# First batch's down-projection sums moved from SBUF to DRAM with accumulating DMAs, and a new set of order offsets

## The chip, the cores and the metric

The kernel runs on one core of one Trainium2 chip. The metric is the device time of one launch in microseconds (us), and what is compared is the median of several runs. A profiled execution is one further launch; its trace gives, for every instruction, the engine, the start, the duration and what ended the idle time before it. TensorE is called PE here, VectorE DVE, ScalarE ACT, GpSimd POOL, and SyncE, which issues nearly all DMAs, SP.

## What is computed

Block-local attention with pooled far keys is followed by a gated feed-forward network. There are 4 batches of 768 tokens, 8 heads of 64, and a hidden width of 1536.

```python
scores_l = scale * np.matmul(q, k.transpose(0, 1, 3, 2))          # only |i-j| < 16 survives the mask
scores_s = scale * np.einsum('bhsd,bhnd->bhsn', q, k_sum) + np.log(block)   # k_sum: max of 32 keys
a = np.exp(scores_all - max); a = a / (sum + 1e-09)               # over both kinds together
x = np.matmul(a, np.concatenate([v, v_sum], axis=2))              # v_sum: mean of 32 values
g = x @ w_gate; silu = g * (1.0 / (1.0 + np.exp(-g)))
out = silu * (x @ w_val) @ w_out
```

The weights come as 64-bit floats. The kernel turns their bits into two float32r parts (high and low), and each product is taken as three matmuls: low by high, high by low, high by high.

## The kernel before

**The program is a list of steps.** `Plan.add` records every step with the engines that may run it, an estimate of its cost on each, and what it reads and writes. `order` then runs a list scheduler (`run`, lines 288 to 388 of the code) over the steps. For each engine it picks the step with the smallest value in the table `late`, which is worked back from when PE wants its operands. `nudge` adds offsets from the table `NUDGES` to that value: `+20.3` makes a step less urgent, `a`, `d` or `p` pins it to ACT, DVE or POOL, and `s1.3` sets how long a PE step of the attention is held back. The engines of the chip then run their own lists strictly in order. A step that waits holds everything behind it on its engine, and a DMA that waits holds the DMAs behind it on SP.

**Work on PE.** Two lists are merged: the feed-forward network (the main line) and the attention of the next batch (the side line). A batch has two halves of 384 tokens (`k` counts halves over all batches: 0 and 1 are batch 0) and four pairs of heads (`u`).

- The side line has the scores `SC(k,u)`, the transposes `PP0/PP1(k,u)` and the attention results `XO(k,u)`.
- Around them stand the pooling of keys and values (`pool`, `vpool`, tiles `ks`, `vr`), maxima and exponentials, the normalisation `nrm` (tile `p`), evictions of the transposes `pt0/pt1`, copies of values (`odd`, `val`, `values`, tile `vw`) and the split of the result into high and low parts `xh/xl` (tiles `xh_B`, `xl_B`).
- In batch 0 the main line does `g(j,hf)` and `v(j,hf)` at line 1014 for each of 12 blocks of hidden units `j` and each half. `silu`, `mul`, `hh`, `hl` follow on the other engines.
- In batches 1 to 3 a seven-product scheme at line 1038 replaces them: `P1(b,j)` to `P7(b,j)`, with sums `s1`, `s7`, `u2`, `vv`, `c12`, `c21`, `c22` taken by ACT, DVE and POOL. `P3` writes over the bank that `vv` reads, so it waits for `vv`.
- After each three `j`, `down` (line 1108) multiplies by `w_out`. For each of six groups of 128 tokens `t`, the steps `D0(b,g,t)` and `D1(b,g,t)` add into one PSUM bank `acc`; `g` is 0 to 3.

**Weights.** In batch 0 each block `j` is decoded: a DMA `raw_w`, then `abs`, `clamp`, `shift`, `sign` (L913), `low` (L919), `hi` and `lo`, after which `w_j` can be used by `g(j,0)`. Four sums `sumA..` follow, and two DMAs `sf(j)` and `wa(j)` keep decoded weights in DRAM. `w_out` is decoded in the same way (`o0` to `o10`). In batch 1, `la(1,j)` and `ls(1,j)` load `wa` and `sf` again, and `sh(j)` and `sl(j)` split the second one. Loads go into four slots, so `ls(1,j)` waits until an earlier block's slot is free.

**Sums of the down-projection.** `finish` (in `down`) takes the bank `acc` when `D1` is done. For `g` = 0 a copy puts it into the SBUF tile `part` (512 floats on 128 partitions, one tile for each `t`). For `g` = 1 to 3, DVE adds `acc` to that tile. After `g` = 3, SP stores the tile to the output. That holds for all four batches. The tiles lie in the pool `late`, which takes the place of the pool `pro` (first batch's data) when its last reader is done.

**Filling matmuls.** The program begins with 11 matmuls of a zero tile (`dummy`, 22 on PE). Before a PE step that the scheduler sees waiting more than half a microsecond in its first 110, `warm_up` puts up to 10 more (20 on PE).

Of the kernel before, what the change touches and what calls it, by code (L numbers as in the profile page):

```python
# [205 lines left out]
XO(0,2) s0.3; raw_w1 +25.9; max1(1,0) +3.5; eps(1,0) +4.9 d; raw_w2 +6.1; sign_w2 -120.3; sumA11_w2 -94.3 d
sumA12_w2 +63.7 p; vw(1,1) +44.9; max0(1,1) +42.9; scl0(1,1) +5.3; eps(1,1) -27.6 d; mul(1,0) +11.9
values(1,0) -18.1 p; pt1(1,0) +7.8 a; xl(0,1) +43.1; max0(1,2) -57.5; scl0(1,2) +130.9; eps(1,2) +44.3
mul(2,0) -15.7; values(1,1) -41 a; XO(1,1) s0.2; xh(1,1) +34 d; xl(1,1) -53.1; max0(1,3) -109.1; exp2(1,3) +22.1
exp3(1,3) +5.5; exp4(1,3) +47.8; eps(1,3) +121.7 p; raw_o0 +23.5; low_o0 +69.4; lo_o0 +58.3 d; raw_o2 +48.5  # L210
clamp_o2 +42.7; sign_o2 +45.2; raw_w3 +21; sumA11_w3 +28 d; sumA12_w3 +25.7 d; hl(0,3,0) -0.6 p; values(1,2) -20.1 a
xh(2,1) -22.5 d; xl(2,1) -26.5; hh(0,3,1) +12.7 d; sumA12_w4 +42.4; raw_o4 +35.9; hh(0,4,0) -12.1 d; kw(2,0) +115.8
vpool(1,0) +88.1; join(2,0) -32.5 p; kt(1,1) +70.8; pool(1,1) +78.9; ttr0(2,0) -54.6; ttr1(2,0) -49.1; SC(2,1) s1.3
ttr0(2,1) -55.2; ttr1(2,1) -123.6; eps(2,1) +41.2 p; silu(4,1) -103.9; mul(4,1) -59.5; hh(0,4,1) -34 d
hl(0,4,1) +64.3 d; clamp_w5 +65.2; shift_w5 +79.9; lo_w5 -50.4 d; wa5 +68.8; hh(0,5,0) +68.1; PP0(2,0) s3
vs(1,0) -17.4; pt1(2,0) +26.7 d; pt0(2,1) -53.5 a; values(2,0) +106.8; values(2,1) +67.6 p; hh(0,5,1) +6.8
vpool(1,2) +63.1; XO(2,0) s0.6; xf(2,0) +17 d; exp4(2,2) -57.9; exp5(2,2) -28.1; exp1(2,3) -93.2; exp2(2,3) -55.9
exp3(2,3) -123.9; exp4(2,3) +44.1; part(0,1,4) +39.9; part(0,1,5) +61.9; abs_w6 +81.1; shift_w6 +15.1
sumA22_w6 -0.2 p; sumA21_w6 +86.8; silu(6,0) +36.6; hl(0,6,0) -20.6 p; pt0(2,3) +18.3 d; PP1(2,3) s1.6
hl(0,6,1) -27.5 d; shift_w7 +106.2; sign_w7 +34.6; sumA11_w7 +27.6 d; sf7 +9.9; q(3,0) -160.7; kw(3,0) -21.8  # L220
join(3,1) +120.2; XO(2,2) s0.3; exp3(3,0) +15.5; ttr1(3,1) +16.1; nrm(3,1) -61.6 p; hh(0,7,1) +47.5 d
hl(0,7,1) +32 p; abs_w8 +79.9; sign_w8 -90.5; low_w8 +35.7; sumA21_w8 -69.7 d; sumA11_w8 -62.6 d; sumA12_w8 +72.7 p
raw_o8 +104; low_o8 +38.2; lo_o8 -29.4 d; silu(8,0) +33.7; hh(0,8,0) +45.2; hh(0,8,1) +73.3; pt0(3,1) -64.1 a
values(3,0) +21.6 d; q(3,3) +60.7; eps(3,2) -90.7 p; ttr1(3,3) +25.6; abs_w9 +28.3; sumA21_w9 -2 p
sumA11_w9 -28.4 p; wa9 +52.2; PP0(3,2) s2.4; values(3,2) +27.9 d; clamp_w10 +53.4; sumA21_w10 -106.3; raw_o10 +41.3
abs_o10 +10.3; clamp_o10 +111.7; shift_o10 +26.9; hh(0,10,1) +50.3 a; lo_w11 +20.7 p; sumA11_w11 -1.8 p
mul(11,0) -71.4; hl(0,11,0) +13; hl(0,11,1) +94.8; T3(1,0) -37; B11h(1,0) -55.1; B11l(1,0) -21.3 p; T2l(1,0) +53 p
T4h(1,0) +126.5; T4l(1,0) -61.4 p; B22h(1,0) -10.2; B22l(1,0) +87; T3(1,1) +75 d; B11h(1,1) -2.1 d; T3h(1,1) +42.1 d
T1h(1,1) +48.7 a; B21h(1,1) -29.9; B22h(1,1) -14.4; sh(0) +44; mul(1,0,0) -83.6 p; hh(1,0,0) -120.5 d
mul(1,0,1) +58.9 p; pool(2,0) +48.2; vpool(2,0) -58.2; q(4,1) +111.3; kw(4,1) +48.8; pool(2,1) +43.5  # L230
# [1170 lines left out]
```

## Time and profile before

| | us |
|---|---|
| median of 3 runs | 687.5 (687.2 to 690.58) |
| the profiled execution's own time | 690.92 |
| its span, from the first to the last instruction | 689.1 |
| PE busy | 673.0 |
| DVE busy | 515.4 |
| ACT busy | 352.0 |
| POOL busy | 96.8 |

HBM was read for 113.73 MB and written for 34.60 MB. The granted PE clock was 0.999. PE's busy time counts the filling matmuls. In a line of the timeline the columns are start, duration, engine, source line, operation and tiles, and in brackets the idle time of the engine just before and what ended it. A group's line gives the count, the busy time, the mean duration in ns and the idle time before.

### The profile page before, as it was taken

How to read it: one execution, taken by the hardware profiler on the slowest of the kernel's cores; microseconds unless marked ns; L12 is line 12 of the kernel's file. 1: busy time of each engine (PE TensorE's matmuls, PEld its weight loads, DVE VectorE, ACT ScalarE, POOL GpSimd, SP SyncE). 2: the span in 40 equal slices, each digit the busy share in tenths (PEclk: the TensorE clock that was granted, in tenths of full speed). 3: DMA queues.
4: the chain of work that ended last, by engine and by line, in shares of the span. 5: the costliest groups of instructions: out<-in, count | busy, mean ns of one | idle time of the engine just before them, and what ended most of it. 6: DMA issues, size and time to landing. Idle time of an engine off the chain costs nothing.

```text
span 689.1 us, 13426 instructions
## 1 busy us (share of the span) xinstructions
PE 673.0 (98%) x5156; PEld 621.2 (90%) x5156; DVE 515.4 (75%) x1141; ACT 352.0 (51%) x855; POOL 96.8 (14%) x109
## 2 busy tenths in 40 slices
...
GB/s 305 299 357 324 255 202 267 163 254 263 246 199 295 204 294 245 233 267 241 289 163 253 201 273 149 231 202 151 235 35 208 193 218 104 214 107 214 107 107 92
DMA packets 69471, 149.19 MB, mean 217 GB/s; under 512 B 22752, under 2 KB 45088, under 8 KB 62496
## 3 DMA queue, kind: packets, MB, share of 16 engines
...
HBM read 113.73 MB, written 34.60 MB: 215 GB/s over the span
## 4 chain that ended last, share of the span: by engine, by line
PE 75%; DMA 10%; DVE 10%; issue 2%; ACT 2%; POOL 1%; SPq 1%; ACTq 0%; POOLq 0%; DVEq 0%
PE p L1038 32%; PE acc L1108 25%; PE g L1014 5%; DMA s<-ss 4%; PE v L1014 4%; PE xo L710 3%; PE sc L561 2%; PE pp L677 2%; DMA sf<-m_w 2%; DMA kt<-in_kP 1%; DVE m_w L919 1%; DVE m_w L913 1%; DMA vt<-in_vT 1%; POOL m_w L447 1%; DMA wa<-wa 1%
## 5 line engine op out<-in xcount | busy, mean ns | idle before, releaser
L1108 PE MATMUL acc<-o,hh 128*128 128x512 f32 x576 | 179.4, 392 | 0.6 <-DVE o L447 0.6
L1108 PEld LDWEIGHTS acc<-o,hh 128*128 128x128 f32 x576 | 107.1, 188 | 23.2 <-DVE o L447 0.9
L1038 PE MATMUL p<-xh_T,s 128*128 128x384 f32 x432 | 122.8, 339 | 1.8 <-DMA s<-ss 1.3
L1108 PE MATMUL acc<-o,hl 128*128 128x512 f32 x288 | 112.5, 391 | 0.0
L1038 PE MATMUL p<-xh_B,wa 128*128 128x384 f32 x288 | 84.8, 335 | 0.0
L442 ACT COPY s<-p 128x384 f32<-128x384 f32 x64 | 30.8, 481 | 102.8 <-PE p L1038 102.8
L1038 PEld LDWEIGHTS p<-xh_T,s 128*128 128x128 f32 x432 | 79.0, 188 | 4.8 <-DMA s<-ss 3.1
L447 DVE TENSOR_TENSOR part<-acc,part 128x512 f32<-128x512 f32 x72 | 47.9, 688 | 33.2 <-PE acc L1108 33.2
L1038 PE MATMUL p<-xl_T,s 128*128 128x384 f32 x216 | 72.2, 334 | 0.0
L1108 PEld LDWEIGHTS acc<-o,hl 128*128 128x128 f32 x288 | 54.0, 188 | 11.5
L1014 PE MATMUL g<-xh_B,w 128*128 128x384 f32 x192 | 53.9, 341 | 3.2 <-DVE w L447 1.7
L604 ACT ACTIVATE p<-p,nm 128x120 f32<-128x120 f32 x144 | 55.1, 384 | 1.1 <-DVE nm L592 0.6
L447 DVE TENSOR_TENSOR c<-p,u 128x384 f32<-128x384 f32 x72 | 39.8, 554 | 20.4 <-PE p L1038 19.9
L447 DVE TENSOR_TENSOR hl<-a,hh 128x384 fp32r<-128x384 f32 x87 | 51.6, 595 | 3.4 <-ACT hh L442 0.6
L442 ACT CAST hh<-a 128x384 fp32r<-128x384 f32 x52 | 26.6, 515 | 53.0 <-DVE a L447 51.5
L1038 PEld LDWEIGHTS p<-xh_B,wa 128*128 128x128 f32 x288 | 53.0, 188 | 0.1
L1014 PE MATMUL v<-xh_B,w 128*128 128x384 f32 x192 | 52.9, 336 | 0.0
L1038 PE MATMUL p<-xl_B,wa 128*128 128x384 f32 x144 | 48.1, 334 | 0.0
L1038 PE MATMUL p<-xh_B,s 128*128 128x384 f32 x144 | 42.6, 336 | 2.1 <-DVE v L447 2.1
L447 DVE TENSOR_TENSOR a<-c,a 128x384 f32<-128x384 f32 x69 | 39.8, 580 | 4.7 <-ACT a L996 2.1
L1038 PE MATMUL p<-xh_T,wa 128*128 128x384 f32 x144 | 42.4, 335 | 0.0
L1038 PEld LDWEIGHTS p<-xl_T,s 128*128 128x128 f32 x216 | 40.6, 188 | 0.3
...
## 6 DMA issues: line engine op xcount, KB each, us to landing
...
s<-ss SPq DMA_DIRECT2D x24, 1024.0 KB, 7.4
raw_w<-in_wgv SPq DMA_DIRECT2D x12, 1024.0 KB, 6.0
ss<-s SPq DMA_DIRECT2D x12, 1024.0 KB, 5.5
...
```

The costliest lines, as they stand in the source:

```text
L442: nc.scalar.copy(out, in_)
L447: vector[e].tensor_tensor(out=out, in0=a, in1=b, op=op)
L561: nc.tensor.matmul(make(sc[h])[s * QT : (s + 1) * QT, c * KC + at : c * KC + at + x.shape[-1]], make(q)[hs, qs], x, start=not biased or c ...
L604: nc.scalar.activation(out=make(p)[:, i, :], in_=make(p)[:, i, :], func=AF.Exp, scale=-1.0, bias=make(nm)[:, i : i + 1], accum_out=make(sm ...
L677: nc.tensor.transpose(make(pp)[:KC, c * P : (c + 1) * P], make(p)[:, g * NT // 2 + c, :], make(id_sb))
L710: nc.tensor.matmul(ps[hs, qs], v, make(pt)[:, h, qs], start=True, stop=True)
L913: lambda e: nc.vector.scalar_tensor_tensor(out=bits(), in0=high(), scalar=-0x40000000, in1=bits(), op0=ALU.bitwise_and, op1=ALU.bitwise_or ...
L919: lambda e: nc.vector.scalar_tensor_tensor(out=bits(), in0=low(), scalar=29, in1=bits(), op0=ALU.logical_shift_right, op1=ALU.bitwise_or), ...
L1014: nc.tensor.matmul(t[:, :TOK], a, x, start=u == 0 and n == 0, stop=u == NP - 1 and n == 2)
L1038: nc.tensor.matmul(t[:, :TOK], a, x, start=first and kk == 0 and n == 0, stop=kk == 1 and n == 2, skip_group_check=not first,)
L1108: nc.tensor.matmul(ps, a, w, start=j == js[0] and m == 0, stop=j == js[-1] and m == 2)
```

## The change

There are four edits.

1. `SPILL = 1`: for batch 0, `finish` copies every `acc` into the SBUF tile (on ACT or DVE) instead of adding on DVE. For `g` = 0 a DMA of SP, `keep(0,t)`, writes the tile to a DRAM tile `sum`. For `g` = 1 to 3 a DMA issued by POOL, `plus(0,g,t)`, adds it to `sum` in DRAM. After `g` = 3, SP copies `sum` to the output. There are 6 `keep`, 18 `plus` and 6 `out` DMAs; batches 1 to 3 stay as they were. The SBUF tile is a new one of the same ring for each `g`, so the copy of one `g` waits until the DMA of the one before has read it.
2. `FIRST`: the scheduler's clocks begin at 5.4 for PE and 1.3 for DMA instead of 0.
3. The scheduler asks for the port shared by DVE and POOL only for steps that use it, since a `plus` does not.
4. Another table `NUDGES`, so that the whole order is another one. `ON_BANK = 2` is what `HALVES` was, and `parts_sb` and `id_r` move to the pool `cst`; neither changes an instruction.

```diff
+SPILL = 1
+ON_BANK = 2
...
+FIRST = {PE: 5.4, DVE: 0.0, ACT: 0.0, POOL: 0.0, DMA: 1.3}
...
+ISSUE = 1.2
...
-kt(0,1) -60.2; id_sb -72.2; vr(1) -12.4; kt(0,0) +8.2; kt(0,2) +20.3; pool(0,2) +97.4; vn(0) +23.7; bias_sb +35.4
+kt(0,1) -75.5; q(0,1) -42.6; raw_parts -146.9; id_sb -68.8; mean_sb -6.3; vn(1) -13.6; vr(1) -11.5; kt(0,3) -18.7
...
-    free = {PE: 0.0, DVE: 0.0, ACT: 0.0, POOL: 0.0, DMA: 0.0}
+    free = dict(FIRST)
...
-                    if x == POOL:
+                    if x == POOL and s.port:
...
+    def add_dma_sum(name, nbytes, out, in_, reads, writes):
+        plan.add(
+            name, {POOL: ISSUE}, lambda e: nc.gpsimd.dma_start(out(), in_(), accum_op=ALU.add), reads, writes, port=False
+        )
+        plan.add(f"{name}'", {DMA: nbytes / 0.33e6}, lambda e: None, reads, writes)
...
+            if b < SPILL:
+                part = buf("late", f"part{t}", [P, DM], f"part_{b}_{g}_{t}", room="late")
+                add_copy(f"part({b},{g},{t})", (ACT, DVE), DM, lambda: make(part), lambda: make(acc), (acc,), (part,), kind="evict")
+                if g == 0:
+                    to = PART[t] = buf("dram", f"sum{t}", [P, DM], f"sum_{b}_{t}")
+                    add_dma(f"keep({b},{t})", P * DM * 4, lambda: make(to), lambda: make(part), (part,), (to,))
+                    return
+                to = PART[t]
+                add_dma_sum(f"plus({b},{g},{t})", P * DM * 4, lambda: make(to), lambda: make(part), (part,), (to,))
+                if g == NJ // GROUP - 1:
+                    add_dma(f"out({b},{t})", P * DM * 4, lambda: out[r : r + P, :], lambda: make(to), (to,), ())
+                return
```

Where the order changes is shown at three places. The first is DVE in the opening stage, from the `sign` of the fourth weight block (tile `m_w_790`) to its `lo` (tile `w_931`), after which PE can begin `g(3,0)`. Before:

```order
L913 SCALAR_TENSOR_TENSOR m_w_790<-raw_w_481,m_w_790 128x1024
L614 TENSOR_REDUCE nm_2_867<-sc_1_2_823 128x3
L919 SCALAR_TENSOR_TENSOR m_w_790<-raw_w_481,m_w_790 128x1024
L447 TENSOR_TENSOR a_1_0_794<-v_0_742,a_1_0_794 128x384
L447 TENSOR_TENSOR xl_B_0_0_929<-xo_0_796,xh_B_0_0_862 128x384
L447 TENSOR_TENSOR m_w_735<-m_w_735 128x256
L444 CAST hh_1_0_937<-a_1_0_794 128x384
L447 TENSOR_TENSOR o_870<-m_o_613,o_870 128x1024
L447 TENSOR_TENSOR w_931<-m_w_790,w_931 128x1024
```

After the change the fourth block's tiles are `m_w_811` and `w_918`; `m_o` belongs to `o2` and `pt_1` to the transposes of `(1,1)`:

```order
L925 SCALAR_TENSOR_TENSOR m_w_811<-raw_w_471,m_w_811 128x1024
L626 TENSOR_REDUCE nm_2_885<-sc_1_2_831 128x3
L931 SCALAR_TENSOR_TENSOR m_w_811<-raw_w_471,m_w_811 128x1024
L453 TENSOR_TENSOR a_1_0_820<-v_0_731,a_1_0_820 128x384
L912 TENSOR_SCALAR m_o_867<-m_o_867 128x1024
L450 COPY pt_1_927<-pp_1_1_914 120x384
L450 COPY pt_1_927<-pp_1_1_920 120x384
L453 TENSOR_TENSOR w_918<-m_w_811,w_918 128x1024
```

The `lo` of `o0` and three small steps have left this stretch, and two evictions of transposes and a `clamp` have come in. On PE, the order here was `SC(1,3)`, `g(3,0)`, `v(3,0)`; now `SC(1,3)` stands between `g(3,0)` and `v(3,0)`.

The second place is DVE in the decoding of the eighth block, between the `shift` and the `lo` of `w7`. `vr_3` is the pooling of the values of `(1,3)`, whose load is `vt_3`; `part_4` and `part_5` release the PSUM banks of `D1(0,1,4)` and `D1(0,1,5)`. Before:

```order
L906 TENSOR_SCALAR m_w_1677<-m_w_1677 128x1024
L447 TENSOR_TENSOR part_3_1390<-acc_1_3_1749,part_3_1390 128x512
L782 TENSOR_REDUCE vr_3_1888<-vt_3_1851 128x24
L913 SCALAR_TENSOR_TENSOR m_w_1677<-raw_w_1449,m_w_1677 128x1024
L447 TENSOR_TENSOR part_4_1395<-acc_1_4_1832,part_4_1395 128x512
L919 SCALAR_TENSOR_TENSOR m_w_1677<-raw_w_1449,m_w_1677 128x1024
L447 TENSOR_TENSOR part_5_1411<-acc_1_5_1853,part_5_1411 128x512
```

After, from `part(0,1,4)` on (`vr_2` is the pooling for `(1,2)`; block `w7` is `m_w_1699`, and its `lo` writes `w_1937`):

```order
L450 COPY part_1_4_1890<-acc_1_4_1833 128x512
L453 TENSOR_TENSOR m_w_1672<-m_w_1672 128x256
L931 SCALAR_TENSOR_TENSOR m_w_1699<-raw_w_1447,m_w_1699 128x1024
L794 TENSOR_REDUCE vr_2_1929<-vt_2_1236 128x24
L665 RECIPROCAL ri_2_1934<-sm_2_1849 128x6
L912 TENSOR_SCALAR m_o_1738<-m_o_1738 128x1024
L450 COPY part_1_5_1942<-acc_1_5_1851 128x512
L918 TENSOR_SCALAR m_o_1738<-m_o_1738 128x1024
L453 TENSOR_TENSOR w_1937<-m_w_1699,w_1937 128x1024
```

The pooling of `(1,3)` no longer stands ahead of `part(0,1,4)` and of the `lo` of `w7`; it comes five rows behind that `lo`.

The third place is SP at the change from batch 0 to batch 1. `wa_2` and `s_2` are the loads `la(1,2)` and `ls(1,2)`. Before:

```order
L461 DMA out<-part_2_1183 128x512
L461 DMA ss_2942<-s_1_2861 128x2048
L461 DMA out<-part_3_1390 128x512
L461 DMA out<-part_4_1395 128x512
L461 DMA out<-part_5_1411 128x512
L461 DMA wa_2_3038<-wa_903 128x1536
L461 DMA s_2_3086<-sf_955 128x1024
```

After:

```order
L467 DMA ss_2907<-s_1_2803 128x2048
L467 DMA out<-sum_0_1157 16x4096
L467 DMA out<-sum_1_1168 16x4096
L467 DMA out<-sum_2_1228 16x4096
L467 DMA out<-sum_3_1387 16x4096
L467 DMA out<-sum_4_1407 16x4096
L467 DMA wa_2_3073<-wa_862 128x1536
L467 DMA s_2_3124<-sf_1127 128x1024
```

Five outputs still stand ahead of the two loads, and each of them now waits for the landing of a `plus` that POOL issues, not for an instruction of DVE; the sixth has moved behind.

More of the change, by code (lines that the diff above doesn't have):

```diff
@@ L206 @@
[L206 to L230, printed above, removed]
@@ L231 @@
-vpool(2,1) +49.5; vw(4,1) +27.4; exp3(4,0) -52.3; ttr1(4,1) -8.9; eps(4,1) -38.4 a; sl(1) -54.9 p; s1(1,1) -3.1 d
-vv(1,1) -37.2; mul(1,1,0) -38.8; c22(1,1) +85.3 d; pool(2,2) -145.4; pool(2,3) -132.1; ls(1,3) +8.5
+kt(0,1) -75.5; q(0,1) -42.6; raw_parts -146.9; id_sb -68.8; mean_sb -6.3; vn(1) -13.6; vr(1) -11.5; kt(0,3) -18.7
+q(0,3) -5.3; kt(0,2) +6.9; pool(0,2) +116.7; vn(0) +8.6; bias_sb -61.1; SC(0,3) s0.4412; exp1(0,3) +173.7
+nrm(0,3) +80.1 p; fv(3) -55.9; exp0(0,0) +98; exp2(0,0) -80.4; exp4(0,0) -50.6; exp5(0,0) -125.4; nrm(0,0) +73.2 p
@@ new lines @@
+rcp(1,1) -90.3; nrm(1,1) -18.5; hh(0,1,0) -12.1 a; hl(0,1,0) +77.7; pt1(1,0) -12 a; xh(0,1) -132.6 a; xl(0,1) -19.5
+SC(1,2) s2.7; max1(1,2) -70.3; exp4(1,2) +179; nrm(1,2) +65; hl(0,2,0) -60.5; pt1(1,1) -109.2 d; xh(1,1) -14.2 d
+scl0(1,3) +9.9; scl1(1,3) +119.9 a; eps(1,3) -116.8 p; nrm(1,3) +2.8 p; raw_o0 +8.4; lo_o0 +62.7; raw_o2 +51.9
+lo_o2 +40.8; raw_w3 +8.7; clamp_w3 -35.3; shift_w3 -13.3; sign_w3 -90.8; hi_w3 -61.1; sumA22_w3 +53.8 p
+hh(0,3,0) +11.9 d; hl(0,3,0) -39 p; PP0(1,2) s2.6; XO(1,2) s0.3391; keep(0,0) -45.2; keep(0,1) -69.7
@@ new lines @@
+hh(0,0,1) +102.5 a; hl(0,0,1) +84.5 d; hh(0,1,1) +14.6 a; hl(0,1,1) -152.2 p; hh(0,3,1) +42.4 a; sumA22_w4 +106.8 d
+sumA21_w4 -74 p; sumA12_w4 +48.4 d; raw_o4 +35.9; shift_o4 -29.8; lo_o4 -99 p; mul(4,0) +4.8; hh(0,4,0) +13.4 d
+pool(1,0) +57.6; vpool(1,0) +64.6; vw(2,0) -50.4; kw(2,1) +60.3; exp5(2,0) +15.8; SC(2,1) s2.5; ttr0(2,1) +31.5
+ttr1(2,1) +35.5; exp0(2,1) +5.2; eps(2,1) -57.3 p; hl(0,4,1) +64.7 d; shift_w5 -67.6; lo_w5 +34.5 p
+sumA22_w5 +15.2 d; silu(5,0) +90.6; PP0(2,0) s0; pt0(2,0) -34.7 d; vs(1,1) -42.2; values(2,1) -81.4 d
@@ new lines @@
+silu(5,1) -69.9; part(0,1,0) +31.5; vpool(1,2) +95.4; vpool(1,3) +133.8; join(2,3) -54.9 d; ttr1(2,2) -24
+eps(2,2) +9.3 p; nrm(2,2) +23.9 p; ttr0(2,3) -21.8; ttr1(2,3) +49.6; eps(2,3) +86.8; rcp(2,3) +56; nrm(2,3) +60.8 p
+part(0,1,4) +3.1 d; plus(0,1,4) -64.6; part(0,1,5) +161.8; sf6 +68.8; shift_o6 +13.3; silu(6,0) +50.4
+hh(0,6,0) -44.6 d; pt0(2,2) -122.8 d; pt1(2,2) +78.6 d; pt0(2,3) -76; abs_w7 +0.5; low_w7 +78.6; sumA21_w7 +98.9 p
+sumA11_w7 +65.3 p; hl(0,7,0) -36 d; q(3,0) +156.4; join(3,0) +41.2; XO(2,2) s0.7; ttr0(3,0) +65.2; ttr1(3,0) -91.8
```

32 lines of the change are left out of this document (22 added, 10 removed).

## The prediction

> **What bounds the kernel now.** I read the page first, then the busy time by stage, then the waits of PE, and last the timeline around each wait and the chain of waits. The page gives the span and the busy time of the engines.
>
> ```profile
> span 689.1 us, 13426 instructions
> PE 673.0 (98%) x5156; PEld 621.2 (90%) x5156; DVE 515.4 (75%) x1141; ACT 352.0 (51%) x855; POOL 96.8 (14%) x109
> ```
>
> PE is busy for 98% of the span, so the kernel as a whole is bound by PE. The change leaves the products as they are, so a gain can only come from the 2% in which PE is idle and from filling matmuls. The windows by stage show where that is. The columns are the window, its length, then busy time and count of PE, PE weight load, DVE, ACT and POOL, the granted clock, the DMA share and GB/s.
>
> ```profile
> 16.40:82.40 66.00, 61.65 (x795) 56.41 (x788) 65.20 (x113) 54.85 (x142) 22.86 (x25) 1.00 0.89 317
> 82.40:230.80 148.40, 146.03 (x1105) 134.38 (x1105) 131.20 (x281) 93.27 (x205) 45.57 (x45) 1.00 0.70 236
> 230.80:377.80 147.00, 144.35 (x1104) 134.09 (x1103) 114.04 (x285) 79.14 (x204) 15.79 (x20) 1.00 0.73 243
> ```
>
> In the opening (16.4 to 82.4) DVE is busy for 65.20 of 66.00 us: there DVE sets the time, and PE's busy time contains filling matmuls. In the rest of batch 0 (to 230.8) PE is idle for 148.40 − 146.03 = 2.37 us, in batch 1 for 2.65 us. Batches 2 and 3 keep their order of work nearly unchanged, and I give them nothing. PE's waits, summed by what ended them, name the pieces (total, times, longest):
>
> ```profile
> PE p L1038 <- DVE v L447: 2.1, 2, 1.4
> PE g L1014 <- DVE w L447: 1.7, 2, 0.9
> PE g L1014 <- DVE part L447: 1.0, 1, 1.0
> PE g L1014 <- ACT a L996: 0.6, 1, 0.6
> ```
>
> All of them are waits for an engine that runs its list in order, so each step that is moved on DVE can shift one of them.
>
> **The change, part by part.**
>
> **1. The opening.** Three rows of DVE's timeline show its two stalls near the start and the `lo` of `w3`; the chain of waits shows the two products of PE that need it.
>
> ```profile
> 13.80 0.95 DVE L500 TENSOR_REDUCE ks<-kt 128x24 f32<-128x768 f32 x1 [1.96 <-DMA kt<-in_kP]
> 16.09 0.29 DVE L444 COPY vs<-pv 24x128 f32<-24x128 f32 x1 [0.36 <-ACT vs L442]
> 62.38 1.21 DVE L447 TENSOR_TENSOR w<-m_w,w 128x1024 fp32r<-128x1024 f32 x1
> ```
>
> ```profile
> 65.15 2.16 PE g L1014 x12
> 67.31 2.08 PE v L1014 x12
> ```
>
> Between the second scale of `(0,3)` and the `lo` of `w3`, DVE's list had 80 steps and now has 85. Twelve have left it: two `nrm` (now on POOL), the pooling of `(1,0)`, three sums `sumA`, one `hh`, three copies of values and two `eps`. Seventeen have come in: four evictions `pt`, seven copies of values, `fv(2)`, a reciprocal, one `sumA`, one `clamp` and two `eps`. The prices, for the stretch from 10 to 66:
>
> ```profile
> L656 DVE TENSOR_TENSOR p<-p,ri 128x720 f32<-128x720 f32 x6 | 5.7, 956 | 0.1
> L447 DVE TENSOR_TENSOR m_w<-m_w 128x256 f32<-128x256 f32 x7 | 2.9, 414 | 0.0
> L444 DVE COPY vw<-vn 64x384 f32<-64x384 f32 x2 | 1.1, 549 | 0.1
> L444 DVE COPY pt<-pp 120x384 f32<-120x384 f32 x1 | 0.6, 551 | 0.0
> L900 DVE TENSOR_SCALAR m_o<-m_o 128x1024 f32<-128x1024 f32 x2 | 1.3, 668 | 0.0
> ```
>
> I set the small ones against each other (two `eps`, `hh` and a sum on the one side, two `eps`, `fv(2)`, the reciprocal and a sum on the other). Out remain 2 x 0.956 + 0.95 (as the pooling at 13.80) + 2 x 0.414 + 3 x 0.549 = 5.3; in come 4 x 0.551 + 7 x 0.549 + 0.668 = 6.7. Net 1.4 us more on an engine that is full. On the other side, the load that DVE awaits at 13.80 is now asked for ahead of one load of `q` (192 KB, an estimate of 0.6 us at the 317 GB/s of the opening), and the copy that waited 0.36 is another one. So the stretch starts about 1.0 earlier and `lo` of `w3` ends 0.4 later. From there PE has the same work, since `SC(1,3)` only changes place with `g(3,0)`. **I take +0.4.** Bounds: −1.0 if the five extra steps only fill gaps, +1.4 if no stall near the start shrinks.
>
> **2. Batch 0's sums.** By the order, 19 of the 24 evictions of `acc` stood on DVE and 5 on ACT; now 7 copies run on DVE and 17 on ACT.
>
> ```profile
> L447 DVE TENSOR_TENSOR part<-acc,part 128x512 f32<-128x512 f32 x72 | 47.9, 688 | 33.2 <-PE acc L1108 33.2
> L442 ACT COPY part<-acc 128x512 f32<-128x512 f32 x21 | 12.0, 587 | 16.6 <-PE acc L1108 15.8
> ```
>
> DVE is freed of 12 x 0.69 = 8.3 us, and ACT takes 12 x 0.587 = 7.0. ACT has 148.40 − 93.27 = 55 us free in that stage, DVE 17: the load itself is covered on both. If that cover is not there, the cost is a later `silu`, such as the 0.6 above. What the freed time is worth stands in PE's waits on DVE there:
>
> ```profile
> 143.21 0.95 DVE L782 TENSOR_REDUCE vr<-vt 128x24 f32<-128x768 f32 x1 [3.06 <-DMA vt<-in_vT]
> 149.91 1.23 DVE L447 TENSOR_TENSOR w<-m_w,w 128x1024 fp32r<-128x1024 f32 x1
> ```
>
> ```profile
> 145.95 0.44 PE L1014 MATMUL g<-xh_B,w 128*128 128x384 f32 x1 [0.98 <-DVE part L447]
> 151.19 0.44 PE L1014 MATMUL g<-xh_B,w 128*128 128x384 f32 x1 [0.80 <-DVE w L447]
> ```
>
> DVE stands 3.06 us for a load of values, and behind it wait `part(0,1,4)`, whose bank PE needs, and the `lo` of `w7`. Now that pooling stands behind both. The one that took its place reads a tile loaded much earlier. **I take −1.8** (0.98 + 0.80); the bound above is 0, if the two `m_o` steps and the DVE `sumA` that came in use up what is won. The 0.6 on ACT stays: 0, bound −0.6.
>
> **3. Eighteen accumulating DMAs from POOL, six `keep` and six `out`.** Of these the trace shows nothing alike: before, POOL issues no DMA of data. Nearest rows:
>
> ```profile
> L447 POOL TENSOR_TENSOR m_w<-m_w 128x256 f32<-128x256 f32 x27 | 27.1, 1005 | 86.5 <-DVE w L447 35.5 <-issue 28.1 <-DVE m_w L447 22.1
> raw_o<-in_wo SPq DMA_DIRECT2D x6, 1024.0 KB, 8.7
> sf<-m_w SPq DMA_DIRECT2D x12, 512.0 KB, 4.9
> out<-part SPq DMA_DIRECT2D x24, 256.0 KB, 2.1
> ```
>
> For one issue on POOL I take 1.0 us, its commonest step: 18 us more on an engine that has 103 us free in that stage and has lost 21 steps to others. For the landing of one `plus` of 256 KB I take 4.9, the row of a 512 KB write, since the tile is also read and added; bounds 2.1 and 8.7. In transfers the sums add 18 x 0.26 = 4.7 MB, and `keep` 1.6 MB, to the 236 GB/s x 148.4 us = 35 MB of that stage: the share of 0.70 would become 0.83, or 0.92 if each sum moves twice. Both are below 1, so 0.
>
> The place where a landing can reach PE is the end of batch 0. The rows are of DVE, SP's queue and PE.
>
> ```profile
> 231.37 1.28 DVE L447 TENSOR_TENSOR part<-acc,part 128x512 f32<-128x512 f32 x2
> ```
>
> ```profile
> 237.22 0.33 SPq L461 DMA_DIRECT2D wa<-wa  x1
> 238.27 0.33 SPq L461 DMA_DIRECT2D s<-sf  x1
> ```
>
> ```profile
> 246.97 0.34 PE L1038 MATMUL p<-xh_T,s 128*128 128x384 f32 x1
> ```
>
> `out(0,4)` waits on SP ahead of `la(1,2)` and `ls(1,2)`, and now for `plus(0,3,4)`. The copy ends at about 232.0, the issue adds 1.0, the landing T, and SP's two issues ahead of `ls` 0.33 each: `ls` could go at 233.7 + T instead of 238.27. Its product begins 0.16 after the last split of that load is done, so PE stalls for T − 4.8: 0.1 at T = 4.9, 0 at 2.1, 3.9 at 8.7. **I take +0.1.** The Trainium skill, page "DMA: Bandwidth & Descriptors", section on the anatomy of one DMA on the GpSimd path, fits such a DMA with 2.0 us plus its bytes at 436 GB/s; that would be 2.6 us for 256 KB (an estimate), and this term 0 instead of 0.1. No run of before shows it, and the fit says nothing of adding.
>
> **4. Batch 1.** DVE at 285 and 318, and PE there:
>
> ```profile
> 285.12 0.70 DVE L444 CAST s<-s 128x1024 fp32r<-128x1024 f32 x1 [2.85 <-DMA s<-sf]
> 318.08 0.95 DVE L500 TENSOR_REDUCE ks<-kt 128x24 f32<-128x768 f32 x1 [2.20 <-DMA kt<-in_kP]
> ```
>
> ```profile
> 286.33 0.45 PE L1038 MATMUL p<-xh_B,s 128*128 128x384 f32 x1 [1.36 <-DVE v L447]
> 287.93 0.45 PE L1038 MATMUL p<-xh_T,s 128*128 128x384 f32 x1 [0.28 <-DVE u L447]
> 319.56 0.44 PE L1038 MATMUL p<-xh_B,s 128*128 128x384 f32 x1 [0.72 <-DVE v L447]
> ```
>
> At 285, `sh(5)` waited 2.85 us for its load ahead of `vv(1,4)`; now `vv` stands ahead of it. But the load comes no sooner, and `P6(1,5)` needs `sl(5)`, so part of the 1.64 returns a few products later: **−0.6**, bounds −1.64 and 0. At 318 the pooling that waits for `kt` stood ahead of `vv(1,6)` alone; now `u2(1,6)` and a reciprocal stand ahead of `vv` too, the first about as long as a copy of 0.55, the second short: **+0.8**, bounds −0.7 (the load comes in time) and +0.8.
>
> **The sum:** +0.4 − 1.8 + 0 + 0.1 − 0.6 + 0.8 = −1.1. The profiled execution took 690.92 us, 3.4 above the median of 687.5 and within the runs shown (687.2 to 690.58) but for 0.3. I apply the difference to the median: **686.4 us**, no change that a measurement could tell; that takes about 0.5%, 3.4 us.
>
> **The rivals.**
>
> *A, faster.* The new list fits throughout: `vv` and the splits at 285 no longer meet, the opening's extra copies lie in gaps, and no DMA is late. Then go 1.0 (opening), 1.8, 0.6 (ACT) and 1.64: −5.0, so 682.5 us. For it speaks that DVE has 8.3 us less in batch 0; against it, that all of PE's idle time from 82.4 to 377.8 is 5.0 us, and that the load behind 285.12 is not earlier.
>
> *B, slower.* The accumulating DMA holds SP at the batch's end. If a `plus` takes twice the 4.9 (the tile moved in two passes), T is 9.8 and PE stalls 5.0 us; the rest of the sum is −1.2, which gives 691.3 us. It decides from T = 4.8 + 1.2 + 3.4 = 9.4 on, which is above the longest median landing of the rows (8.7 for four times the bytes). For it speaks that five such DMAs stand in a row there; against it, that every row of 256 to 512 KB is well below.
>
> *C, slower.* The opening gets longer. Its DVE is full, two `nrm` run on POOL, and a POOL step that shares DVE's port slows it. The rows:
>
> ```profile
> L656 POOL TENSOR_TENSOR p<-p,ri 128x720 f32<-128x720 f32 x5 | 7.5, 1508 | 12.5 <-DVE ri L653 11.7 <-DVE sm L650 0.8
> 60.70 1.75 DVE L447 TENSOR_TENSOR o<-m_o,o 128x1024 fp32r<-128x1024 f32 x1
> ```
>
> With no earlier start the net is 1.4; each `nrm` is 1.508 − 0.956 = 0.55 later, 1.1 in all; and if five of the 1.2 us steps each take 0.5 longer, as the one at 60.70 (1.75 beside 1.21 at 62.38), 2.5 more: +5.0, less 1.5 elsewhere, 691.0 us.
>
> That the change doesn't do what it says is ruled out by the order: 18 DMAs stand on POOL and no add of batch 0 on DVE.
>
> **How the numbers follow.** Forecast 0.46, A 0.32, B 0.12, C 0.10: of the terms, the two largest gains are read from waits whose cause has moved, and the losses are prices of steps on a full engine, so that the gain's side has more of the rest. A is the only case beyond −3.4: faster 0.32, same 0.46, slower 0.22. The range begins at 681.8, where all lower bounds are met together (−1.0 − 1.8 − 0.6 − 1.6 − 0.7 = −5.7), and ends at 692.0, just above B and C, whose unknown sizes reach little further before they grow improbable.
>
> **What would show it.** Each step can be read in the profile of the changed kernel. The end of `v(3,0)` was at 67.31 + 2.08 = 69.4 and should be near 70. The waits of PE on `part` and `w` at the eighth block should be gone. SP should issue `ls(1,2)` within 0.3 of where PE's progress allows it, with a landing of `plus` near 5; a landing over 9 means B. PE's wait for `v` near 285 should shrink, and that near 318 grow. The prediction is wrong if PE's idle time from 82.4 on changes by more than 3 us, or if `v(3,0)` ends before 68 or after 71.5.

## The result and the profile after

The changed kernel takes 698.76 us (median of 6 runs, 694.83 to 701.14) against 687.36 for the kernel before. The ratio is 1.015 with a 95% interval of 1.0125 to 1.0175. By the medians it is slower by 11.4 us (1.5%), outside the range that was given. The profiled execution took 701.14 us, 10.2 more than that of before (690.92).

The page's first lines after the change:

```profile
span 699.3 us, 13462 instructions
PE 675.2 (97%) x5132; PEld 622.3 (89%) x5132; DVE 516.0 (74%) x1154; ACT 359.3 (51%) x865; POOL 97.2 (14%) x106
```

The windows by stage, cut at the same times as those of before:

```profile
16.40:82.40 66.00, 59.09 (x725) 53.83 (x724) 60.49 (x107) 49.87 (x135) 19.20 (x20) 0.97 0.84 291
82.40:230.80 148.40, 144.07 (x1116) 132.21 (x1117) 129.92 (x283) 96.64 (x209) 44.51 (x46) 1.00 0.85 267
230.80:377.80 147.00, 143.49 (x1051) 132.30 (x1051) 110.88 (x281) 83.25 (x206) 19.34 (x22) 0.99 0.77 245
377.80:689.10 311.30, 308.28 (x1994) 285.90 (x1990) 204.33 (x467) 124.24 (x297) 13.43 (x16) 1.00 0.50 173
```

Two columns changed character. The DMA share of the second stage rose from 0.70 to 0.85, as the prediction said (0.83), and PE nevertheless lost time there: it is idle for 4.33 us instead of 2.37. The granted clock, 1.00 everywhere before, is 0.97 and 0.99 in two stages. DVE is no longer full in the opening (60.49 of 66.00 us), so it is not the amount of work on DVE that makes the opening longer.

PE's waits name other engines and tiles than before:

```profile
PE xo L722 <- DVE pt L450: 3.2, 2, 2.2
PE p L1050 <- DMA s<-ss: 3.0, 3, 1.7
PE xo L1168 <- ACT p L640: 2.4, 1, 2.4
PE p L1050 <- DVE v L453: 2.3, 1, 2.3
PE p L1050 <- DVE s L453: 1.3, 1, 1.3
```

The waits of `g` on `w` and `part` at the eighth block are gone, as forecast. In their place stand the results `xo` (at 27.0, at 63.7, where fillings stand ahead of it, and at 167.7), the product that waits for `v` at the start of batch 1, and `s` near 298. The row of `s<-ss` belongs to batches 2 and 3.

To see where the 10.2 us arise, the ends of the same PE steps are compared, read from the timelines of the profiled executions (us; differences to before). The last four columns are runs told below.

| end of step | before | changed | changed, again | `order_only` | `order_only_both` | `both_moved` |
|---|---|---|---|---|---|---|
| `v(0,1)`, end of the opening | 86.39 | +3.8 | +3.8 | +3.4 | +1.7 | +1.3 |
| `v(3,1)` | 105.05 | +5.9 | +5.9 | +5.5 | +2.1 | +1.6 |
| `D1(0,1,5)` | 140.79 | +5.9 | +5.9 | +5.5 | +2.1 | +1.6 |
| `v(8,1)` | 172.87 | +7.1 | +7.2 | +3.1 | −0.3 | +2.3 |
| `D1(0,3,5)`, end of batch 0 | 230.93 | +6.7 | +7.2 | +2.2 | −1.2 | +2.1 |
| `P7(1,2)` | 250.25 | +10.7 | +9.0 | +2.2 | −1.2 | +2.1 |
| `D1(1,3,5)`, end of batch 1 | 390.08 | +8.8 | +6.8 | +0.5 | −3.7 | +1.2 |

Each column is one execution. How much one can differ shows `before_moved` (run 9): up to `v(0,1)` it has the order of the kernel before, and ends that step 1.6 us later, with a granted clock of 0.50 from 33.6 to 37.0.

Four losses can be told apart: 3.8 us in the opening, 2.1 behind `v(2,1)`, about 4 in group 2 of batch 0 (the difference of the changed kernel to `order_only`, which has the same order, grows from 0.4 to 4.5), and 4.0 or 1.7 at the start of batch 1. Gains lie between them.

### The profile page after: what moved, and what is told of

It reads as the page before. It is cut to its first block, busy times and chain, and to the rows that moved or that the text cites. A ratio compares the mean times of both kernels' runs of the same rounds, so it can differ in the third digit from the quotient of the medians.

```text
span 699.3 us, 13462 instructions
## 1 busy us (share of the span) xinstructions
PE 675.2 (97%) x5132; PEld 622.3 (89%) x5132; DVE 516.0 (74%) x1154; ACT 359.3 (51%) x865; POOL 97.2 (14%) x106
## 3 DMA queue, kind: packets, MB, share of 16 engines
q0 software_dynamic: 2592, 4.72, 4.2%
## 4 chain that ended last, share of the span: by engine, by line
PE 73%; DMA 11%; DVE 7%; issue 4%; ACT 2%; POOL 2%; SPq 0%; POOLq 0%; ACTq 0%; DVEq 0%
PE p L1050 32%; PE acc L1120 24%; PE v L1026 4%; PE g L1026 4%; DMA s<-ss 4%; DMA sf<-m_w 3%; PE sc L573 3%; PE xo L722 2%; DMA s<-sf 2%; PE pp L689 2%; DMA sum<-part 1%; DMA raw_w<-in_wgv 1%; DMA q<-in_qP 1%; ACT m_w L908 1%; DVE m_w L925 1%
## 5 line engine op out<-in xcount | busy, mean ns | idle before, releaser
L453 DVE TENSOR_TENSOR part<-acc,part 128x512 f32<-128x512 f32 x54 | 36.2, 688 | 29.7 <-PE acc L1120 29.7
```

The costliest lines, as they stand in the source:

```text
L453: vector[e].tensor_tensor(out=out, in0=a, in1=b, op=op)
```

## The experiments

In the diffs, functions and names are those of the changed kernel. `order_only`, `plain_write`, `no_group_1` and the runs with `order_only` in their name leave sums out, as their expectations say; their times stand for the order and the transfers.

**1. The changed kernel once more (`after_again`).** No edit.

> The changed kernel once more, to see which of its losses recur. If the losses come from the order, g(0,1) starts again near 85.8 (before: 82.0), and P3(1,1) at the start of batch 1 again waits over 2 us. If one of them was chance, it is gone or in another place. Median 696 to 701 either way.

Measured: 697.64 us, ratio 1.0136 (1.0107 to 1.0166). The opening, the loss behind `v(2,1)` and that in group 2 recur within 0.2 us (table). The wait at the start of batch 1 recurs with 1.3 instead of 2.3 us. In batches 2 and 3 the two profiled runs drift 2.7 us apart, mostly in waits for loads of `s`; that did not recur and is not explained here.

**2. The same order without the DMAs (`order_only`).**

```diff
-                    add_dma(f"keep({b},{t})", P * DM * 4, lambda: make(to), lambda: make(part), (part,), (to,))
+                    plan.add(f"keep({b},{t})", {DMA: P * DM * 4 / 0.33e6}, lambda e: None, (part,), (to,))
...
+                store = lambda e: nc.sync.dma_start(out[r : r + P, :], make(part)) if last else None
-                add_dma_sum(f"plus({b},{g},{t})", P * DM * 4, lambda: make(to), lambda: make(part), (part,), (to,))
+                plan.add(f"plus({b},{g},{t})", {POOL: ISSUE}, store, (part,), (to,), port=False)
```

> The changed kernel with every instruction in the same order on PE, DVE, ACT and POOL, but without keep and plus; the last group's tile is stored where its plus stood. It leaves out the first three groups' sums of batch 0. If the DMAs are what costs (traffic, and SP held by the out DMAs), what is lost behind v(3,1) goes: about 6 us less than the changed kernel, 692 to 693, with only the opening's 3.8 us left. If the order is what costs, only the stall of 4 us at the start of batch 1 goes, since SP is free there: 694 to 695, and the waits of the results of (2,2) at 165 and of D0(0,0,3) at 98 stay.

Measured: 689.15 us, ratio 1.0014 (0.9992 to 1.0035). Of the slowdown, 8.5 to 9.6 us go with the 24 DMAs. In the opening, where none of them runs, and behind `v(2,1)` the loss stays; in group 2 and at the start of batch 1 it goes. The order costs 5.5 us up to `v(3,1)` and gains 5.0 from there to the end of batch 1.

**3. Writing without adding (`plain_write`).**

```diff
-            name, {POOL: ISSUE}, lambda e: nc.gpsimd.dma_start(out(), in_(), accum_op=ALU.add), reads, writes, port=False
+            name, {POOL: ISSUE}, lambda e: nc.gpsimd.dma_start(out(), in_()), reads, writes, port=False
```

> The changed kernel with each plus as a plain write from the same queue, without adding; it leaves out the sums over the groups in batch 0. If adding is what makes the DMA slow, the landing falls from 6.6 us towards 2.5 (the keep DMAs of the same size), the queue's share of the engines halves from 4.2%, and the wait of P3(1,1) goes: about 695. If issuing from POOL makes it slow, landing and time stay as they are: 698 to 700.

Measured: 691.1 us, ratio 1.0055 (1.0033 to 1.0076): 6.5 to 7.7 us less than the changed kernel, 2 more than without the DMAs. The queues and DMA issues of the changed kernel (packets, MB, share of 16 engines; then KB and us to landing):

```profile
q0 software_dynamic: 2592, 4.72, 4.2%
sum<-part POOLq DMA_DIRECT2D x18, 256.0 KB, 6.6
sum<-part SPq DMA_DIRECT2D x6, 256.0 KB, 2.5
out<-sum SPq DMA_DIRECT2D x6, 256.0 KB, 4.4
```

The same of the run that writes plainly:

```profile
q0 software_dynamic: 1440, 4.72, 1.9%
sum<-part POOLq DMA_DIRECT2D x18, 256.0 KB, 3.6
```

Adding takes the same 4.72 MB through 2592 packets instead of 1440, more than twice the engines' time, and 3.0 us more to land. So it is the adding, and not POOL's queue, that makes most of the cost; 2 us remain with plain writes.

**4. The old table with the DMAs (`spill_old_order`).**

```diff
-FIRST = {PE: 5.4, DVE: 0.0, ACT: 0.0, POOL: 0.0, DMA: 1.3}
+FIRST = {PE: 0.0, DVE: 0.0, ACT: 0.0, POOL: 0.0, DMA: 0.0}
```

The table `NUDGES` is that of the kernel before as well.

> The kernel before with edits 1 and 3 alone: the old table and the old initial clocks, with the sums in DRAM. Up to the first part DMAs its order is that of before. If the DMAs cost by themselves, it takes 4 to 6 us more than before, 691 to 693, with a stall where batch 1 begins. If the loss lies in the new order alone, it stays within 2 us of 687.4.

Measured: 708.45 us, ratio 1.0295 (1.0247 to 1.0342), far beyond both expectations. It doesn't isolate the DMAs: with the DMA steps in the list the scheduler makes a third order from the first group's copies on, in which `g` waits 6.4 us for `w` on DVE and 2.1 for `w` on POOL. What it shows is that the old offsets don't carry over to the new list of steps.

**5. The opening without seven fillings (`no_fill`).**

```diff
-        if s.engine == PE and s.start < 110.0:
+        if s.engine == PE and s.start < 110.0 and s.name != "XO(1,1)":
```

> The changed kernel without the seven fillings (14 on PE) ahead of XO(1,1). In the changed kernel they start only when the bank of that step is free, at 63.74, and last until 67.10. If they are what costs in the opening, XO(1,1) starts near 64 and g(0,1) 2 to 3 us earlier than 85.8, and the whole falls by 2 to 3 us to about 695.5. If the late operands or DVE's longer list are what costs, g(0,1) moves by less than 1 us, since XO(1,1) and g(3,0) then run at the lower clock or wait themselves.

Measured: 694.82 us, ratio 1.0105 (1.0074 to 1.0137); the end of `v(0,1)` is 0.4 us later than before instead of 3.8. PE in the changed kernel at that place, and the granted clock around it:

```profile
63.74 3.36 PE L1168 MATMUL xo<-warm 128*128 128x128 f32 x14 [2.44 <-ACT p L640]
67.03 0.38 PE L722 MATMUL xo<-pt,vw 120*64 120x64 f32 x4
```

```profile
60.00:64.00 4.00, 1.56 (x11) 1.28 (x10) 4.00 (x7) 3.99 (x15) 0.00 (x0) 0.97 0.99 398
64.00:66.00 2.00, 2.00 (x10) 2.00 (x11) 1.43 (x3) 1.07 (x5) 1.50 (x1) 0.50 0.36 147
66.00:68.00 2.00, 2.00 (x31) 1.71 (x29) 0.00 (x0) 1.29 (x2) 0.74 (x2) 0.71 0.78 307
```

The same place without the fillings:

```profile
63.64 0.57 PE L722 MATMUL xo<-pt,vw 120*64 120x64 f32 x12 [2.30 <-ACT p L640]
```

```profile
63.60:65.00 1.40, 1.36 (x27) 1.29 (x28) 1.40 (x3) 0.88 (x5) 0.46 (x1) 1.00 0.41 170
```

The fillings write into the bank of the step that they stand ahead of, and that bank is freed by an exponential on ACT. So they don't fill the wait; they begin when it ends, at 63.74, when the operands of `XO(1,1)` are there too, and here they run at half the clock: 3.36 us for 14. That clock is a cost of its own. The same place in two other runs, `late_out` with the fillings (clock 1.00) and `three_repairs` without them (clock 0.50 from 63.8 to 67.2):

```profile
64.22 1.83 PE L1168 MATMUL xo<-warm 128*128 128x128 f32 x14 [3.05 <-ACT p L640]
```

```profile
64.80 0.69 PE L1026 MATMUL g<-xh_B,w 128*128 128x384 f32 x1
```

The times from the end of this wait to the end of `v(3,0)`, in the profiled executions of all runs with this order, part the two (us):

| | clock stayed at 1.00 | clock fell to 0.50 |
|---|---|---|
| with the fillings | 9.18 (`order_only`, `plain_write`, `late_out`) | 10.66 to 10.73 (changed kernel, its repeat, `no_group_1`) |
| without them | 7.39 to 7.42 (`no_fill`, `both_moved`, `order_only_both`) | 8.91 to 8.96 (`three_repairs`, `pool_moved`, `order_only_moved`) |

The fillings cost 1.8 us and the clock 1.5, each with or without the other. The profiled run of `no_fill` had neither, and that its clock did not fall was chance: three of the six runs without the fillings lost it all the same.

The length of the wait does not decide it either. It was 2.06 to 2.76 us where the clock fell and 2.11 to 3.05 where it did not. In the trace of the changed kernel the clock stays at 1.00 for 58.03 us ahead of this fall and for 187.73 to the next one, 17 and 55 times 3.41 us, and in all these traces each stretch at 0.50 inside the program lasts 3.41 us or twice that. So here the clock changes on a grid of 3.41 us. In the changed kernel the whole wait of 2.44 us lay in one cell of it (60.34 to 63.75) and the clock fell at its end; in `late_out` a boundary at 62.91 parted the 3.05 us into 1.74 and 1.31, and it did not fall. How much idle time of a cell is enough is not shown.

**6. The outputs later on SP (`late_out`).**

```diff
+    outs = [s for s in todo if s.name.startswith("out(0,")]
+    todo = [s for s in todo if s not in outs]
+    at = next(i for i, s in enumerate(todo) if s.name == "ls(1,4)")
+    todo[at + 1 : at + 1] = outs
```

> The changed kernel with the six out(0,t) issued behind ls(1,4) on SP, nothing else moved. If SP held by the out DMAs is what stalls P3(1,1), its wait (2.3 and 1.3 us in two profiles) and the slow clock behind it go, and the whole falls by 1.7 to 4 us, to 694 to 697. If it is the traffic of the accumulating DMAs that makes the load of sf late, the landing of that load stays over 6 us and most of the wait stays.

Measured: 699.38 us, ratio 1.0153 (1.0109 to 1.0198; runs from 693.35 to 702.53): no gain that can be told in the whole. In its place the edit does what was expected: PE reaches `P7(1,2)` 11.6 us later than before, as it did the end of batch 0, so nothing is lost at the start of batch 1. The profiled run had lost 5.8 us behind `v(2,1)` instead of 2.1, which the edit does not touch; its clock was at 0.50 from 100.5 to 107.3. The start of batch 1 in the changed kernel, SP, DVE and PE:

```profile
237.48 8.78 SPq L467 DMA_DIRECT2D out<-sum  x4
246.70 0.35 SPq L467 DMA_DIRECT2D wa<-wa  x1
247.17 0.36 SPq L467 DMA_DIRECT2D s<-sf  x1
```

```profile
253.83 0.69 DVE L450 CAST s<-s 128x1024 fp32r<-128x1024 f32 x1 [4.05 <-DMA s<-sf]
254.44 0.55 DVE L453 TENSOR_TENSOR v<-p,s 128x384 f32<-128x384 f32 x1
```

```profile
255.05 0.69 PE L1050 MATMUL p<-xh_B,s 128*128 128x384 f32 x1 [2.26 <-DVE v L453]
...
258.55 0.33 PE L1050 MATMUL p<-xh_T,s 128*128 128x384 f32 x1
```

```profile
255.00:256.50 1.50, 1.45 (x5) 1.45 (x6) 1.50 (x2) 1.50 (x9) 0.00 (x0) 0.50 1.01 398
256.50:258.00 1.50, 1.50 (x6) 1.50 (x6) 1.46 (x5) 0.43 (x3) 0.00 (x0) 0.50 0.62 254
```

SP stands at the four `out` until 246.3, and `la` and `ls` follow. DVE waits for that load with `vv(1,1)` behind it, PE waits 2.26 us for `vv`, and then runs at half the clock for 3 us: matmuls of 0.69 and 0.52 us where the same ones take 0.33. `P3(1,1)` and `P6(1,2)` occupy PE 1.75 us longer than before. Wait and clock make the 4.0 us.

**7. Without one group's DMAs (`no_group_1`).**

```diff
+                if g == 1:
+                    plan.add(f"plus({b},{g},{t})", {POOL: ISSUE}, lambda e: None, (part,), (to,), port=False)
...
+                    return
```

> The changed kernel without the six plus of group 1; it leaves those sums of batch 0 out. Every engine keeps its order. If the accumulating DMAs hold up the ordinary ones, the six issues of SP from kw(3,1) to sf6 take 3 us instead of 9, ACT's wait of 6.8 us for sf6 ahead of abs_w8 goes, XO(2,2) no longer waits for 2.2 us, and the whole falls by about 3.5 us to 695. If that wait has another cause (the load of vt or the order), it stays.

Measured: 692.55 us, ratio 1.0085 (1.0052 to 1.0119), 5.1 to 6.2 us less than the changed kernel by the medians. From `D1(0,1,5)` to `v(8,1)` its profiled run takes 3.6 us less. Abs of `w8` starts at 154.97 without a wait, and `XO(2,2)` has none. SP in the changed kernel, and behind it ACT, DVE and PE:

```profile
141.09 3.65 SPq L467 DMA_DIRECT2D kw<-in_kP  x2
144.84 2.00 SPq L467 DMA_DIRECT2D wa<-w  x1
146.89 3.09 SPq L467 DMA_DIRECT2D q<-in_qP  x2
150.02 0.46 SPq L467 DMA_DIRECT2D vt<-in_vT  x1
150.59 0.45 SPq L467 DMA_DIRECT2D sf<-m_w  x1
```

```profile
160.24 1.16 ACT L908 ACTIVATE m_w<-raw_w 128x1024 f32<-128x1024 f32 x1 [6.79 <-DMA sf<-m_w]
```

```profile
158.73 0.95 DVE L794 TENSOR_REDUCE vr<-vt 128x24 f32<-128x768 f32 x1 [4.93 <-DMA vt<-in_vT]
```

```profile
167.71 0.28 PE L722 MATMUL xo<-pt,vw 120*64 120x64 f32 x2 [2.18 <-DVE pt L450]
```

The same place in the run without any of the DMAs (`order_only`), SP and ACT:

```profile
140.69 1.90 SPq L467 DMA_DIRECT2D kw<-in_kP  x2
143.81 0.53 SPq L467 DMA_DIRECT2D wa<-w  x1
144.39 1.59 SPq L467 DMA_DIRECT2D q<-in_qP  x2
...
146.89 0.42 SPq L467 DMA_DIRECT2D sf<-m_w  x1
```

```profile
152.93 1.14 ACT L908 ACTIVATE m_w<-raw_w 128x1024 f32<-128x1024 f32 x1
```

While `plus(0,1,t)` run, SP's own issues become slow: `kw` 3.65 us for two instead of 1.90, `wa` 2.00 instead of 0.53. `sf6` goes out 3.7 us later, lands 9.6 us after its issue instead of 4.9, and its tile is not free until 160.2. ACT, which needs that tile for `w8`, stands for 6.8 us, DVE 4.9 us for `vt`, and both are late for `XO(2,2)`. The windows from 140 to 152, of the changed kernel and of `order_only`, show it as a whole:

```profile
140.00:152.00 12.00, 12.00 (x109) 10.91 (x106) 11.67 (x38) 9.48 (x32) 9.21 (x10) 1.00 1.09 256
```

```profile
140.00:152.00 12.00, 12.00 (x103) 10.98 (x96) 11.67 (x37) 9.31 (x31) 5.65 (x5) 1.00 0.90 274
```

With the adding DMAs the share is higher (1.09 against 0.90) and less is moved (256 against 274 GB/s). A share above 1 means that the times of packets overlap, so it is not the used part of a capacity. Nor does it tell the harm alone: with plain writes the same window has 1.04 at 342 GB/s, SP's two `kw` take 1.21 us, and ACT waits 1.3 us for `sf6`.

**8. The new table without the DMAs (`no_spill_no_fill`).** `SPILL = 0`, the offsets of `keep` and `plus` skipped, and the edit of run 5.

> The new table and the new initial clocks with the sums in SBUF as before, and without the fillings ahead of XO(1,1). If the DMAs and these fillings are all that costs, and the new order by itself is worth about 3 us behind the opening, it comes to 685 to 687, level with before or faster. If the fillings don't matter, 688 to 690.

Measured: 702.59 us, ratio 1.021 (1.0191 to 1.023). Neither case: as in run 4 the scheduler makes another order, in which PE waits 7.0 us for the normalisation `p` on DVE. Runs 4 and 8 say nothing of the DMAs; they show that an order must be kept fixed to study one part of a change.

**9. Three steps moved in the kernel before (`before_moved`).**

```diff
+    for name, behind in [('vpool(1,3)', 'lo_w7'), ('sh(5)', 'vv(1,4)'), ('pool(3,2)', 'vv(1,6)')]:
...
+        todo.remove(s)
+        todo.insert(next(i for i, x in enumerate(todo) if x.name.replace(" ", "_") == behind) + 1, s)
```

> The kernel before with three steps moved back on DVE and nothing else: vpool(1,3) behind the lo of w7, sh(5) behind vv(1,4), pool(3,2) behind vv(1,6). If PE's waits there were priced rightly in the prediction (0.98 and 0.80, 1.36, 0.72), they go and the kernel takes up to 3.9 us less, 683.5 to 685.5. If what waits for the same loads is only late in turn, the waits come back a few products later and the time stays at 687.

Measured: 685.03 us, ratio 0.9964 (0.9948 to 0.9979), faster than both kernels. DVE there:

```profile
149.15 1.22 DVE L447 TENSOR_TENSOR w<-m_w,w 128x1024 fp32r<-128x1024 f32 x1
150.28 0.94 DVE L782 TENSOR_REDUCE vr<-vt 128x24 f32<-128x768 f32 x1
```

```profile
283.06 0.56 DVE L447 TENSOR_TENSOR v<-p,s 128x384 f32<-128x384 f32 x1 [0.52 <-PE p L1038]
283.53 0.68 DVE L444 CAST s<-s 128x1024 fp32r<-128x1024 f32 x1
```

Once nothing stands behind them, the pooling and the split no longer wait, and PE's waits at `g(6,1)`, `g(7,0)`, `P3(1,4)` and `P3(1,6)` are gone. The whole gains 3.0 of the 3.9 us by the medians, 2.5 by the ratio.

**10. Three repairs (`three_repairs`).** The edits of runs 5 and 6, and on ACT abs of `w4` moved behind `hh(0,1,1)`.

> The changed kernel with the three places mended that the profiles name outside the DMAs' traffic: no fillings ahead of XO(1,1) (3.4 us), abs of w4 behind hh(0,1,1) on ACT (up to 2 us), and the six out DMAs behind ls(1,4) on SP (1.7 to 4 us). If these add up, it takes 690 to 692, and what is left over before is what the accumulating DMAs' traffic costs in group 2, 3.5 us, less what the new order gains. If the traffic costs more than that, it stays over 693.

Measured: 695.22 us, ratio 1.0094 (1.0057 to 1.0131). The start of batch 1 costs nothing, but behind `v(2,1)` 3.5 us are lost instead of 2.1: abs of `w4` alone was not what held `D0(0,0,3)`. In its place `pool(1,3)` waited 3.36 us on DVE ahead of `hl(0,0,1)`.

**11 and 12. Two poolings moved (`pool_moved`, `order_only_moved`).** The edits of runs 5 and 6 (of run 5 alone on top of `order_only`), with `pool(1,2)` behind `hl(0,0,1)` and `pool(1,3)` behind `mul(2,1)`; abs of `w4` where the changed kernel has it.

> The changed kernel without the fillings ahead of XO(1,1), with the out DMAs behind ls(1,4), and with two poolings of keys moved back on DVE: pool(1,2) behind hl(0,0,1), pool(1,3) behind mul(2,1). abs of w4 is where the changed kernel has it. If these poolings, which wait 1.8 and 1.0 us for their loads (3.4 in the run with three repairs), are what makes D0(0,0,3) late, the 2 to 3.5 us lost between v(2,1) and v(3,1) go, and it takes 691 to 693. If hl(0,1,1) on POOL is what makes it late, at most 1 us goes, and it stays near 695.

> The run without keep and plus (it leaves out the first three groups' sums of batch 0), with the same two poolings moved and without the fillings ahead of XO(1,1). If the new order is worse than the old one only by these two places, it falls by 4 to 5 us from 689.2, to 684 to 685.5, below before; what the accumulating DMAs cost is then the difference to the run with the poolings moved, 7 to 8 us. If the fillings and poolings only hide other waits, it stays at 687 to 689.

Measured: 696.88 us, ratio 1.0125 (1.0093 to 1.0156), and 691.28, ratio 1.0052 (1.0032 to 1.0071). Both were worse than hoped: the loss behind `v(2,1)` grew to 6 us. `kt(1,3)` needs the slot that `pool(1,2)` frees, and `raw_w4` stands behind `kt(1,3)` on SP; so a later pooling made the load of `w4` later, and abs of `w4` waited 5.9 and 6.8 us for it on ACT, ahead of `hh(0,1,1)`. Of the 6 us PE's own wait there is 2.9 and 3.8; the rest is mostly the clock, at 0.50 from 99.5 to 106.4 and from 102.3 to 105.7. The theory of the poolings alone falls, as that of abs of `w4` alone had.

**13 and 14. Both loads' readers moved (`both_moved`, `order_only_both`).** The same bases, with abs of `w4` behind `silu(2,1)`, and its clamp and `pool(1,3)` behind `mul(2,1)`; `pool(1,2)` stays.

> The changed kernel without the fillings ahead of XO(1,1), with the out DMAs behind ls(1,4), and with every step that waits for the loads of w4 and of kt(1,3) moved behind what D0(0,0,3) needs: abs of w4 behind silu(2,1) on ACT, its clamp and pool(1,3) behind mul(2,1) on DVE. If these two loads together are what makes D0(0,0,3) late, the loss between v(2,1) and v(3,1) falls below 1 us and the kernel takes 691 to 693. If it is something else (hl(0,1,1) on POOL), 2 us stay there and it takes 694 to 696.

> The same moves in the run without keep and plus (it leaves out the first three groups' sums of batch 0), with the stores where that run has them. If the new order's own losses are these two places, it falls from 689.2 to 684 to 686, and the difference to the run with the DMAs, 6 to 8 us, is what the accumulating DMAs cost. If other waits take their place, it stays at 687 or above.

Measured: 691.42 us, ratio 1.0072 (1.0043 to 1.01), and 686.24, ratio 0.9986 (0.997 to 1.0002). The loss behind `v(2,1)` is 0.4 us in both. Two loads held two engines there, and only moving the readers of both helps. The difference of the two runs, 5.2 us, is what the DMAs still cost when the outputs no longer hold SP at the start of batch 1: 3.0 us from `D1(0,1,5)` to `v(8,1)`, where ACT again waits 6.3 us for `sf6`, and most of the rest in batch 1, where `P6(1,5)` waits 2.2 us instead of 0.3.

## Why the prediction was wrong

**What bounds the kernel** was read rightly: the change could only move waits of PE. But it was summed as if each wait cost its idle time and no more. After 2.44 and 2.26 us of idleness PE ran at half the granted clock for 3.4 us. In the profile of before no row shows that: its longest wait of PE behind the start is 1.61 us, at 32.21. That this was safe was luck, since `before_moved` has the same wait of 1.61 us at 33.05, and its clock fell at 33.56. Over all runs the granted clock is 0.992 in mean for the changed kernel and 0.994 for its repeat, against 0.998 for the 23 runs of before beside it. Over the span that is 5.4 and 4.4 us of work against 1.7, so about 3 of the lost us are slow clock (an estimate, as if PE had work all that time). The Trainium skill, page "TensorE: Matmul & The Clock Gate", part 1, says that the clock is halved after an idle window of about 3.4 us and is whole again after as long a busy one. The return agrees here (0.50 from 63.75 to 67.17 and from 254.90 to 258.31); the fall came after less. After 2.18 us (ahead of 167.71), 2.30 (in `no_fill`) and 3.05 (in `late_out`) it did not come: the wait's place on the grid told, not its length alone (run 5).

**Term 1, the opening (+0.4), failed** at the sentence "From there PE has the same work". DVE's part was right: the `lo` of `w3` ended at 64.4, the forecast gave 64.0. But PE reached `g(3,0)` only at 67.93, and `v(3,0)` ended at 74.5 where the forecast said 70, since `XO(1,1)` stands ahead of `g(3,0)` with fillings that wait for the bank. They cost 1.8 us, and the clock behind the wait 1.5. The order showed the fillings; I counted only DVE's list. The loss behind `v(2,1)`, 2.1 us, was not in the sum at all: it is two loads that are awaited at the head of ACT and of DVE.

**Term 2 (−1.8) was right.** The waits at `g(6,1)` and `g(7,0)` are gone, and `before_moved` shows them worth what the rows said, where only the pooling was moved: its profiled run gains 2.4 us from `D1(0,1,5)` to `v(8,1)`. It reached that place 3.2 us later than before, so that part of the 2.4 may be loads that were there in time for that reason.

**Term 3, the accumulating DMAs (0 and +0.1), failed twice**, and this is the larger part. "Both are below 1, so 0" took the mean share over 148 us for what happens where the DMAs run: from 140 to 152 the share is 1.09 with less moved than without them. What suffers is whoever waits behind: SP's issues, the landing of `sf6` (9.6 us instead of 4.9), then the steps at the head of ACT's and DVE's lists. At the end of batch 0 the mechanism and its arithmetic were right and the landing was mis-sized: 6.6 us instead of 4.9. The prediction's `ls` at 233.7 + T, moved by the 6.7 us that PE was late, is 247.0; it went at 247.17. T − 4.8 gives 1.8; the wait was 2.26, and the slow clock added 1.75. The `plus` that `out(0,4)` waited for landed 7.3 us after its issue (238.44 to 245.76), so agreement to 0.2 us with the median landing is in part luck. That is rival B, at a landing of 6.6 instead of its 9.4. In the repeat the same wait was 1.34 us and the clock did not fall, so the place cost 1.7 us there. The Trainium skill's fit, page "DMA: Bandwidth & Descriptors", section on the anatomy of a DMA on the GpSimd path, gave an estimate of 2.6 us; 3.6 were measured for the plain write and 6.6 with adding.

**Term 4.** The −0.6 near 285 came about in part, as −0.4 (1.26 us at `P6(1,5)` in place of 1.36 and 0.28 at two products). The +0.8 near 318 did not: the load was there in time and the wait went. This is the bound below that I had named.

**The rivals.** B had the right place and the wrong threshold. C had the right stage and the wrong engine: neither the two `nrm` on POOL nor DVE's port made the opening longer. A does not hold even for the order alone with two faults mended: `order_only_both` is 3.7 us ahead of before at the end of batch 1 by the profiles, but that execution of before was 3.6 us slower than the median of before, and by the medians the run is only level with or just below before (0.9986).

Nearly all of the loss is thus found by experiment: 1.8 us are the fillings and 1.5 the slow clock behind the same wait, 1.7 to 2.1 two loads at the heads of their engines, 1.7 to 4.0 SP and the clock behind it, about 5 the traffic of the adding DMAs, less some 3 to 5 that the new order gains. The shares are not quite additive, and part of them is the clock, which falls in one execution and not in the next. The runs of the changed kernel spread over 6 us, so no single share is known to better than 1 or 2 us.
